# Fourier mixing followed by an ELU layer: the order of the first seven steps rewritten as one list of single operations

## The chip, the cores and the metric

The kernel runs on one core of a Trainium2 chip. The metric is device time in microseconds (us), the median over runs of the whole kernel. Before the change it is 1950.72 us, the median of three runs (1949.22 to 1950.72). The profile shown below is of one more execution; its run took 1951.19 us and its span, from the first to the last instruction, is 1949.1 us.

## The reference

```python
def _attn_ref(x):                      # x: (8, 3008, 256) float32
    X = np.fft.fft(x, axis=1)
    X = np.fft.fft(X, axis=2)
    return X.real.astype(np.float32)

def _moe_ref(x, w_in, w_out):          # x: (24064, 256), w_in: (256, 2048), w_out: (2048, 256)
    h = x @ w_in
    g = np.where(h > 0.0, h, np.exp(np.minimum(h, 0.0)) - 1.0)
    return (g @ w_out).astype(np.float32)
```

The two weight matrices arrive as 8-byte floating-point numbers, because they are scaled by a NumPy double. The kernel converts them to float32 itself, by integer operations on the two 32-bit words of each number.

## The kernel before, in words

**The mathematics.** The transform over 256 channels is multiplied into w_in (the "fold" of a chunk of w_in), so that what remains for x is the transform over 3008 rows. Its symmetries cut it to quarters: x is first folded into sums and differences of mirrored rows and channels (`fold_x`, L498; all VectorE at the start), and four half-length transforms of each batch are matmuls against constant matrices (`Dft`, L609). The results go into rings `Rr`, `Ir` and `Rb` in SBUF, 256 columns to a tile. A **step** (or slot) then takes one tile and 256 of the 2048 hidden channels: two matmul groups give h for a frequency and for its mirror, ELU is applied to both, and a third group multiplies by w_out. There are 47 tiles and 8 steps to a tile, 376 steps. The first sixteen steps go back and forth between tiles 0 and 1; from step 16 on a step uses a form with fewer products.

**Names.** The change gives each operation a short name; they are used here for both kernels. For step n:

- Pn (TensorE, L794): the cosine part of h into a new PSUM bank with the tag `H`. Vn (VectorE, L803): E = P plus a rank-one term. Qn (TensorE, L799): the sine part, added onto P in the same bank, so it waits for Vn, which reads the bank first.
- hn (VectorE, L817): h of the mirror. b+n and b-n (ScalarE, L842, L846): what lies below zero. x+n and x-n (ScalarE): exponentials. g+n and g-n (VectorE, L857, L861): ELU. g+n is the last reader of the step's `H` bank.
- Xan and Xbn (TensorE, L904): the products with w_out, eight matmul records each.

For the first batch: the names x, R, I, O, J are five transforms (of the extra channel, and the four of `R_even`, `I_even`, `R_odd`, `I_odd`), each with -even and -odd (matmuls), -copy (ScalarE), -sum, -up and -down (VectorE; -up and -down write the ring). e0 to EO3 are the folds of x, c0 to c3 one-column copies, xs four tiny sums. For chunk c of w_in (w) and of w_out (u): a and b take bits out of the high words (VectorE), p, l, d convert (ScalarE), s sets the sign (VectorE), R adds and M multiplies (GpSimd, but VectorE for w0), P makes sum and difference for the fold (GpSimd). fc is the fold of w chunk c (TensorE, into an `H` bank), Wsc and Wcc copy it out (ScalarE), wmc and wexc turn one row of it into columns. L0 to L3 are loads of the second batch.

**Banks.** `bank` (L404) gives PSUM banks by tag: one each for pA, pB, pC, pD and M, three for `H`. P, f, the two halves of J and a few later operations share the three `H` banks; a fourth user waits until a bank's last reader is done.

**What sets the order.** Every compute operation is pinned: each engine executes its instructions in the order in which the program emits them. The emission order is that of the events: `at(t, fn)` (L1131) notes a function with a number, and L1434 calls them in the order of the numbers. The numbers stand for microseconds of a plan in which a step takes `PERIOD` = 4.8; no time is enforced. For the beginning they are written in several places: L1146 to L1184 (folds, first transforms, chunks 0 and 1), the table `first` (L1204) for the chunks, L1222 to L1231 for the folds, the table `begin` for steps 0 and 1 (L1247, L1258), and L1345 on with two calls of `at_half` for the O and J transforms. A single event often emits several operations: `fields` is a and b, `power` is p, l and d, `fold_now` a whole string of folds. SyncE issues the loads in a fixed order, and `load_rest` (L1135) holds the later ones back until x has landed. Before any of this, 46 dummy matmuls are issued.

Of the kernel before, what the change touches and what calls it, by code (L numbers as in the profile page):

```python
# [25 lines left out]
NE = 377  # L26
# [80 lines left out]
def kernel(  # L107
# [109 lines left out]
    class Chunk:  # L217
# [30 lines left out]
        def fields(self):  # L248

            if not wide:  # L250
                return
            lo, hi, dst = self.parts()
            t = spool.tile([128, 512], I32, tag=self.tmp_tag, bufs=1, name="pow2")
            self.t = t.rearrange("p (a b) -> p a b", a=dst.shape[1])
            pin(
                nc.vector.tensor_scalar(
                    out=self.t, in0=hi, scalar1=0x7FF00000, scalar2=None,
                    op0=ALU.bitwise_and,
                )
            )  # L260
            pin(
                nc.vector.tensor_scalar(
                    out=dst.bitcast(I32), in0=hi, scalar1=0xFFFFF, scalar2=0x100000,
                    op0=ALU.bitwise_and, op1=ALU.bitwise_or,
                )
            )

        def power(self):

            if not wide:  # L270
                return
            act(self.t, self.t, func=AF.Relu, scale=8.0, bias=ebias)
            if self.shared:
                lo, _, dst = self.parts()
                act(lo.bitcast(FP), lo.bitcast(U32), scale=2.0**-52)
                act(dst, dst.bitcast(I32), scale=2.0**-20)

        def round(self):

            if not wide:  # L280
                return
            lo, hi, dst = self.parts()
            if self.shared:
                gtt(dst, lo.bitcast(FP), dst, ALU.add)
                return
            pin(
                nc.vector.scalar_tensor_tensor(
                    out=dst, in0=lo.bitcast(U32), scalar=2.0**-32,
                    in1=dst.bitcast(I32), op0=ALU.mult, op1=ALU.add,
                )  # L290
            )

        def pair(self):

            dst = self.dst()
            gtt(self.ab[:, 0:256], dst[:, 0], dst[:, 1], ALU.add)
            gtt(self.ab[:, 256:512], dst[:, 0], dst[:, 1], ALU.subtract)

        def scale(self):

            self.multiply()
            if self.pairs:
                self.pair()

        def multiply(self):
            if not wide:
                return
            lo, hi, dst = self.parts()
# [5 lines left out]
            )  # L314
            if self.shared:
                gtt(dst, dst, self.t.bitcast(FP), ALU.mult)
                return
# [4 lines left out]
                )  # L322
            )
# [124 lines left out]

    def put_chunk(c):
        cols = slice(c * 256, (c + 1) * 256)  # L450
        for n, dst in enumerate((Ws, Wc)):
            act(dst[:, cols], folds[c][:, 256 * n : 256 * n + 256])
# [45 lines left out]
    def fold_x(L, engine_of, pieces):  # L498
# [3 lines left out]
        def op(key, o, a, b, f):  # L502
# [3 lines left out]
            n = o.shape[1]  # L506
            cuts = [n * i // pieces for i in range(pieces + 1)]
            for i in range(pieces):
# [100 lines left out]
    class Dft:  # L609
# [30 lines left out]
        def minus(self):  # L640
# [8 lines left out]
            if self.ri == 0 and not self.kodd and not self.first:  # L649
                vtt(R4[:, self.b : self.b + 1], u[:, 0:1], v[:, 0:1], ALU.subtract)  # L650
# [165 lines left out]

    def h_minus(i):  # L817
        S = steps[i]
        S.G = spool.tile([128, GW], FP, tag="G", bufs=3, name="G")
# [22 lines left out]
    def below_plus(i):  # L842
        S = steps[i]
        below(S.G[:, 512:1024], S.H)
# [262 lines left out]
    for load in loads[:5]:  # L1107
# [8 lines left out]
        L_first, lambda key: nc.vector, 1  # L1116
    )

    def fold_now(keys):
        for key in keys.split():  # L1120
            ops[key, 0]()
# [13 lines left out]
    def load_rest():  # L1135
# [7 lines left out]
        for chunk in (w1_chunks[3], w2_chunks[1], w1_chunks[4], w2_chunks[2]):  # L1143
            chunk.load()

    at(-26.9, lambda: fold_now("e3 c3 o3"))  # L1146
    at(-26.8, w1_chunks[0].fields)
    at(-26.7, w1_chunks[0].power)
    at(-26.6, w1_chunks[0].round)
    at(-26.5, w1_chunks[0].scale)  # L1150
    at(-26.4, lambda: fold_now("e0 c0 e2 c2 E2"))
# [3 lines left out]
    at(-25.5, load_rest)  # L1155
    at(-24.5, begin_x_even)
    at(-24.4, lambda: fold_now("e1 c1 E0 EO0"))
    at(-20.7, lambda: load_mats(1, 1))
    at(-20.6, w1_chunks[5].load)
    at(-20.5, w2_chunks[5].load)  # L1160
    at(-13.2, lambda: fold_chunk(0))
    at(-13.1, lambda: put_chunk(0))
    at(-13.1, lambda: dft_now(state["x_even"], 0, "pC"))
    at(-13.09, lambda: state["x_even"].copy())
    at(-13.08, lambda: dft_now(state["x_even"], 1, "pD"))
    at(-13.0, lambda: dft_now(R_even, 0, "pA"))
    at(-12.9, lambda: dft_now(R_even, 1, "pB"))
    at(-11.1, lambda: fold_now("o0 o2 O2 o1 O0 EO2"))
    at(-11.0, lambda: state["x_even"].unfold())
    at(-10.95, R_even.copy)  # L1170
    at(-10.94, R_even.unfold)
    at(-10.9, R_even.plus)
    at(-10.89, lambda: state["x_even"].plus())
    at(-10.885, lambda: act(Ir[96:128, 0:NE], Rb[96:128, 0:NE]))
    at(-10.88, w1_chunks[1].fields)
    at(-10.87, w1_chunks[1].power)
    at(-10.86, w1_chunks[1].round)
    at(-10.85, R_even.minus)
    at(-10.5, lambda: dft_now(I_even, 0, "pC"))
    at(0.05, lambda: dft_now(I_even, 1, "M"))  # L1180
    at(0.6, lambda: state["x_even"].minus())
    at(0.61, lambda: act(Ir[96:128, NE:RUN], Rb[96:128, NE:RUN]))
    at(-10.84, w1_chunks[1].scale)
    at(1.3, lambda: fold_now("EO1"))  # L1184

    T = PERIOD
    for chunk, k in (
        (w2_chunks[0], 0),
        (w1_chunks[2], 1),
        (w2_chunks[1], 2),  # L1190
        (w1_chunks[3], 3),
        (w2_chunks[2], 4),
        (w1_chunks[4], 5),
        (w2_chunks[3], 6),
# [9 lines left out]
        first = (  # L1204
            (0.96, 0.96, 0.97, 1.9),
            (2.1, 2.9, 2.91, 4.22),
            (2.95, 2.96, 2.97, 4.2),
            (0.95, 0.96, 0.97, 4.2),
        )
        dt = first[k] if k < 4 else (-0.5, 0.05, 0.06, 2.95)  # L1210
        for d, fn in zip(dt, (chunk.fields, chunk.power, chunk.round, chunk.scale)):
            at(t + d, fn)
    for chunk, t in (
        (w2_chunks[3], 0.5),
        (w2_chunks[4], 0.95),
# [6 lines left out]
    for c in range(1, 8):  # L1222
        at((2 * c - 2) * T + 4.7 if c > 1 else 2.7, lambda c=c: fold_chunk(c))
        t = (2 * c - 1) * T + 0.03 if c > 1 else 3.0
        at(t, lambda c=c: put_chunk(c))
        if c > 1:
            at(t + 0.01, lambda c=c: spread_last_row(c))
    at(-10.6, lambda: turn_last_row(0))
    at(-10.59, lambda: put_last_row(0))
    at(3.15, lambda: turn_last_row(1))  # L1230
    at(T + 0.25, lambda: put_last_row(1))  # L1231
    for i in range(8):
        at((12.9 + 0.5 * i) * T + 3.6, lambda i=i: sum_weights(i))
    at(2 * T + 4.2, lambda: fold_now("EO3"))
# [9 lines left out]
    for slot in range(total):  # L1244
        i = slot % 2 * 8 + slot // 2 if slot < 16 else slot
        t = slot * T
        begin = (  # L1247
            (0.0, mm_P),
            (0.4 if slot == 0 else 0.9, even_part),
            (2.17, mm_Q),  # L1250
            (3.55, h_minus),
            (4.2, below_plus),
            (4.8, below_minus),
            (T + 0.01 if slot < 16 else T + 1.5, exp_plus),
            (T + 0.02 if slot < 16 else T + 2.21, exp_minus),
        )
        if slot == 1:
            begin = (  # L1258
                (0.1 - T, mm_P),
                (0.7 - T, even_part),  # L1260
                (2.6 - T, mm_Q),
                (1.5, h_minus),
                (2.95, below_plus),
                (3.0, below_minus),
                (3.01, exp_plus),
                (3.02, exp_minus),
            )

        X3 = ((3 * T + 0.1 if i % 8 == 0 else 2 * T + 3.05, mm_X3),)
        for dt, fn in begin + (  # L1270
            (T + 2.2, g_plus),
            (T + 2.9, g_minus),
        ) + (
            (
                (2 * T + 0.87, lambda i: mm_plain(i, 0)),
                (2 * T + 3.04, lambda i: mm_plain(i, 1)),
            )
            if i < 16
            else WINOGRAD + X3
        ):  # L1280
            at(t + dt, lambda fn=fn, i=i: fn(i))
# [59 lines left out]
    def begin_folds(b):  # L1341
        state["EO"], state["ops"] = fold_x(state["L"], lambda key: nc.gpsimd, 2)

    steps_b = HALF * 8 // TW
    for t, fn in (  # L1345
        (-1.8, I_even.copy),
        (0.5, I_even.unfold),
        (0.55, I_even.plus),
        (0.65, I_even.minus),
        (3.1, lambda: dft_now(R_odd, 0, "pA")),  # L1350
        (3.2, lambda: dft_now(R_odd, 1, "pB")),
        (T + 0.005, R_odd.copy),
        (T + 1.9, R_odd.unfold),
        (T + 4.2, R_odd.plus),
        (T + 4.21, R_odd.minus),
    ):
        at(t, fn)
    at_half(3, lambda: I_odd, 0, 0)
    at_half(5, lambda: I_odd, 1, HALF)
# [25 lines left out]
    for b in range(1, NB):  # L1385
# [4 lines left out]
        for n in range(6):  # L1390
            t = l0 + gap * n if n < 4 else l0
            at(t * T + 0.2, lambda n=n: state["loads"][n]())
# [73 lines left out]
```

## Time and profile before

| | |
|---|---|
| median of three runs | 1950.72 us (1949.22 to 1950.72) |
| profiled span | 1949.1 us |
| busy | TensorE 1935.8, GpSimd 1376.4, VectorE 1299.4, ScalarE 864.8 us |
| first matmul of the fold of chunk 0 | 13.43 us from the span's start |
| P0, P2, P6, P7 start | 25.40, 39.95, 67.87, 74.16 us |
| last matmul starts | 1945.8 us |

How to read it: TensorE is busy nearly all of the span by its own records, but a matmul's record is longer than the time to the next one's start, so short pauses do not show as idle. A stretch of the timeline tells more: a row has the start, the time to the end of the last of its instructions, the engine (PE is TensorE, DVE VectorE, ACT ScalarE, POOL GpSimd), what is written and read, and in brackets the idle time before it with what ended it. Four matmul records of 256 columns in a row take 0.86 us, eight take 1.73 us.

### The profile page before, as it was taken

The page shows a single profiled execution, that of the slowest core. Times are in us where ns is not written, and L with a number is a line of the kernel's source. Part 1 is how long each engine was busy: PE and PEld are TensorE (multiplying, and loading weights), DVE is VectorE, ACT ScalarE, POOL GpSimd, SP SyncE. Part 2 cuts the span into 40 slices and gives each one's busy share as a digit, 9 for nine tenths or more (in the row PEclk, how much of TensorE's full clock was granted, in tenths as well). Part 3 has the DMA queues.
Part 4 walks back from the last instruction along what each step waited for, and adds up shares of the span by engine and source line. Part 5 has one row for each costly group of instructions (what it writes and reads, how often), then busy time and mean ns, then how long its engine had stood idle before and what let it go on. Part 6 is the DMA issues. An engine that isn't in the chain of part 4 may idle for free.

```text
span 1949.1 us, 26994 instructions
## 1 busy us (share of the span) xinstructions
PE 1935.8 (99%) x8912; PEld 1653.3 (85%) x8912; DVE 1299.4 (67%) x2396; ACT 864.8 (44%) x1671; POOL 1376.4 (71%) x1816
## 2 busy tenths in 40 slices
PE   8999999999999999999999999999999999999999
PEld 5788788888888888888888888888888888888887
DVE  7966666666667666666666665676666766667666
ACT  4654444444444444444344444444444444344443
POOL 3887767776678766777677876778767776456655
PEclk9999999999999999999999999999999999999999
DMA  8246120101101021010210202012020010100101
GB/s 310 66 32 49 29 54 20 47 14 26 42 20 44 15 44 28 18 47 13 53 24 12 49 10 59 12 20 58 7 54 11 20 23 14 17 12 11 23 9 25
DMA packets 263290, 70.25 MB, mean 36 GB/s; under 512 B 248606, under 2 KB 249522, under 8 KB 263152
## 3 DMA queue, kind: packets, MB, share of 16 engines
q1 hardware_dynamic: 257360, 55.69, 15.0%
q0 software_dynamic: 3616, 12.59, 2.1%
q8 instruction: 70, 1.15, 0.3%
q14 instruction: 68, 0.56, 0.1%
q10 hardware_dynamic: 2176, 0.26, 0.1%
HBM read 43.66 MB, written 24.80 MB: 35 GB/s over the span
## 4 chain that ended last, share of the span: by engine, by line
PE 94%; DVE 2%; POOL 2%; ACT 1%; DMA 1%; issue 1%; SPq 0%; DVEq 0%
PE H L410 38%; PE pB L410 16%; PE pC L410 16%; PE pD L410 16%; PE pA L410 8%; POOL WT L419 1%; POOL G L419 0%; DMA xl<-in_x_dram 0%; DVE E L811 0%; POOL w L419 0%; DVE G L837 0%; DVE o L504 0%; DMA xl<-in_x_dram,ix 0%; DVE e L504 0%; DVE v L416 0%
## 5 line engine op out<-in xcount | busy, mean ns | idle before, releaser
L419 POOL TENSOR_TENSOR G<-G 128x256 f32<-128x256 f32 x1440 | 1034.8, 728 | 510.7 <-DVE G L837 341.2
L811 DVE SCALAR_TENSOR_TENSOR E<-Rb,wex,H 128x256 f32<-128x256 f32 x752 | 327.9, 477 | 541.3 <-PE H L410 537.2
L422 ACT ACTIVATE G<-H 128x512 f32<-128x512 f32 x376 | 224.5, 597 | 958.9 <-DVE G L821 958.9
L410 PE MATMUL H<-Ir,Ws 128*128 128x256 f32 x1504 | 387.6, 380 | 5.3 <-DVE E L811 4.3
L410 PE MATMUL H<-Rr,Wc 128*128 128x256 f32 x1504 | 386.8, 380 | 0.0
L410 PE MATMUL pC<-G,WT 128*128 128x256 f32 x1440 | 369.5, 379 | 0.0
L410 PEld LDWEIGHTS H<-Rr,Wc 128*128 128x128 f32 x1504 | 284.8, 190 | 55.3 <-issue 3.0
L410 PEld LDWEIGHTS H<-Ir,Ws 128*128 128x128 f32 x1504 | 278.5, 189 | 54.1 <-DVE E L811 6.0
L410 PEld LDWEIGHTS pC<-G,WT 128*128 128x128 f32 x1440 | 273.6, 190 | 37.2
L821 DVE SCALAR_TENSOR_TENSOR G<-E,H 128x512 f32<-128x512 f32 x376 | 256.9, 683 | 41.2 <-POOL G L419 5.0
L837 DVE SCALAR_TENSOR_TENSOR G<-G,H 128x512 f32<-128x512 f32 x376 | 255.9, 681 | 42.5 <-ACT G L422 42.5
L837 DVE SCALAR_TENSOR_TENSOR G<-M,G 128x512 f32<-128x512 f32 x376 | 256.8, 683 | 0.0
L422 ACT ACTIVATE G<-G 128x512 f32<-128x512 f32 x376 | 233.2, 620 | 0.0
L410 PE MATMUL pD<-G,w 128*128 128x256 f32 x784 | 229.4, 379 | 0.8 <-POOL G L419 0.8
L410 PE MATMUL pA<-G,w 128*128 128x256 f32 x784 | 229.3, 379 | 0.0
L410 PE MATMUL pB<-G,w 128*128 128x256 f32 x784 | 229.2, 379 | 0.0
L422 ACT ACTIVATE M<-G 128x512 f32<-128x512 f32 x376 | 224.3, 596 | 0.0
L422 ACT ACTIVATE M<-M 128x512 f32<-128x512 f32 x376 | 220.9, 588 | 0.0
L410 PE MATMUL pB<-G,WT 128*128 128x256 f32 x720 | 214.8, 380 | 0.3
L410 PE MATMUL pD<-G,WT 128*128 128x256 f32 x720 | 214.1, 379 | 0.0
L410 PEld LDWEIGHTS pD<-G,w 128*128 128x128 f32 x784 | 148.9, 190 | 21.4 <-POOL G L419 1.2
L410 PEld LDWEIGHTS pA<-G,w 128*128 128x128 f32 x784 | 148.9, 190 | 20.4 <-issue 0.2
(148 smaller groups left out, 1415.3 us busy)
## 6 DMA issues: line engine op xcount, KB each, us to landing
out_dram<-ot SPq DMA_DIRECT2D x496, 32.0 KB
xl<-in_x_dram SPq DMA_DIRECT2D x16, 512.0 KB
xl<-in_x_dram SPq DMA_DIRECT2D x16, 256.0 KB
out_dram<-ot SPq DMA_DIRECT2D x256, 2.0 KB
Rb<-r SPq DMA_DIRECT2D x10, 376.0 KB
raw<-in_moe_w_in_dram SPq DMA_DIRECT2D x7, 512.0 KB
MC<-dft_mats SPq DMA_DIRECT2D x3, 943.5 KB
raw<-in_moe_w_out_dram SPq DMA_DIRECT2D x4, 512.0 KB
```

Of the source, the lines that this page charges most:

```text
L410: nc.tensor.matmul(out_, lhsT=lhsT, rhs=rhs, start=start, stop=stop, skip_group_check=True)
L419: pin(nc.gpsimd.tensor_tensor(out=o, in0=a, in1=b, op=op))
L422: pin(nc.scalar.activation(out=o, in_=i, func=func, **kw))
L811: nc.vector.scalar_tensor_tensor(out=S.E[:, c], in0=Rb[:, cols(i)], scalar=wex[:, f : f + 1], in1=S.H[:, c], op0=ALU.mult, op1=ALU.add,)
L821: nc.vector.scalar_tensor_tensor(out=two(S.G[:, 0:512])[:, :, ::-1], in0=two(S.E), scalar=2.0, in1=two(S.H), op0=ALU.mult, op1=ALU.subtract,)
L837: nc.vector.scalar_tensor_tensor(out=o, in0=e, scalar=-1.0, in1=h, op0=ALU.add, op1=ALU.max)
```

## The change

- The operations of the beginning are split into single ones: `fields` becomes `top` and `mantissa` (a, b); `power` becomes p, l and d; `scale` becomes s, M and P; the fold's two copies become two operations; R's one-column subtraction is taken out of `minus` and becomes R4.
- A list `FRONT` of 40 lines names 227 operations, in the order in which they are to be emitted. It replaces all numbers of the places above up to about step 6. What comes later keeps its place, except that chunk 4 of w_out is loaded a little later, and a few chunks' conversions come earlier.
- The folds e0 and e2 are cut in two, rows 0 to 3 and 4 to 5, because the two parts of these tiles come by separate transfers. The first batch's other folds stay whole.
- J-even is emitted directly behind Q1 and ahead of P2, J-odd behind P2 and wm1; before, they came after Xb1 and Xb3. J-up and J-down stay behind step 6.

The core of the diff (the list is cut to the lines that the text speaks of):

```diff
-    def fold_x(L, engine_of, pieces):
+    def fold_x(L, engine_of, cuts_of):
...
-            cuts = [n * i // pieces for i in range(pieces + 1)]
-            for i in range(pieces):
+            cuts = cuts_of(key, o.shape[1])
+            for i in range(len(cuts) - 1):
...
     EO, ops = fold_x(
-        L_first, lambda key: nc.vector, 1
+        L_first,
+        lambda key: nc.vector,
+        lambda key, n: (0, 4, n) if key in ("e0", "e2") else (0, n),
     )
...
-    at(-26.9, lambda: fold_now("e3 c3 o3"))
-    at(-26.8, w1_chunks[0].fields)
...
-    at(0.05, lambda: dft_now(I_even, 1, "M"))
...
+    FRONT = (
+        (-20.44, "e3 o3"),
+        (-18.71, "w0a w0b w0p w0R c3"),
+        (-17.22, "w0s e0a"),
+        (-15.57, "w0M e2b e2a"),
+        (-14.12, "e0b o2 o0"),
+        (-12.44, "f0 O2 xl1 c0"),
+        (-11.12, "e1 c2 Wc0 xs"),
+        (-9.82, "c1 E2 x-even E0"),
+        (-8.33, "x-odd w1b EO0"),
+        (-6.77, "o1 R-even w1a w2l O0"),
+        (-5.15, "R-odd Ws0 w1l u0b EO2 w1p"),
+        (-3.54, "R-copy EO1 w1d I-odd x-copy R-sum w1R u0d"),
+        (-2.11, "x-sum R-up I-even x-up"),
+        (-0.66, "w2b Irc u0a P0 w1s I-copy u0p"),
+        (0.64, "R4 I-sum w1M wm0 u0l O-even R-down I-up wex0"),
+        (2.2, "V0 u0R P1 x-down w4l"),
+        (3.47, "w2a Q0 w1P w2d Irc2 O-odd V1 O-copy"),
+        (4.86, "b+0 I-down w2R w2p h0 x+0"),
+        (6.34, "EO3 f1 u1l b-0 Q1 u1b"),
+        (7.71, "u2l u0s J-even Wc1 w2s x-0"),
+        (9.1, "O-sum Ws1 w2M P2 g-0 J-copy u1d h1 wm1 b+1"),
+        (10.2, "u0M O-up J-odd g+0 x+1 u1a wex1 b-1 w2P x-1"),
+        (11.39, "Xa0 g+1 w3l O-down u1R u1p V2 f2 g-1"),
+        (12.84, "w3a Q2 w4b u1s Xb0 w3b b+2 u1M u2b"),
+        (14.05, "w3d Ws2 P3 x+2 J-sum w3R w3p h2 Xa1"),
+        (15.67, "Wc2 V3 b-2 u2a x-2 w3s Q3"),
...
+        (21.24, "Q4 L1 g-3 u2p f3 h4 b+4 u2R"),
+        (22.53, "u3d g+3 Xb2 b-4 u2s Ws3 Wc3 w4s"),
...
+        (32.99, "h6 u3M g+5 b-6 J-up"),
+        (34.63, "J-down"),
+    )
+    front = set()
+    for t, line in FRONT:
+        for n, name in enumerate(line.split()):
+            front.add(name)
+            at(t + 0.001 * n, names[name])
...
-        (3.1, lambda: dft_now(R_odd, 0, "pA")),
-        (3.2, lambda: dft_now(R_odd, 1, "pB")),
...
-    at_half(3, lambda: I_odd, 0, 0)
-    at_half(5, lambda: I_odd, 1, HALF)
```

## The prediction

> **What bounds the kernel now.** I read the page first, then busy time by stretch, then the timeline of TensorE and of VectorE over the first 70 us. From the page:
>
> ```profile
> PE 1935.8 (99%) x8912; PEld 1653.3 (85%) x8912; DVE 1299.4 (67%) x2396; ACT 864.8 (44%) x1671; POOL 1376.4 (71%) x1816
> ```
>
> TensorE is the bound of the whole, and the change neither adds nor removes a matmul. The time can only change by pauses of TensorE, and only early ones are touched. Busy time by stretch (start:end, length, then busy us and instructions of PE, weight loads, DVE, ACT, POOL; granted clock; DMA share; GB/s):
>
> ```profile
> 13.40:25.40 12.00, 10.23 (x52) 7.02 (x51) 11.65 (x21) 1.76 (x6) 0.00 (x0) 1.00 1.03 403
> 25.40:40.00 14.60, 12.29 (x48) 7.66 (x47) 10.89 (x26) 8.62 (x20) 6.54 (x6) 0.88 0.88 317
> 40.00:44.80 4.80, 3.83 (x18) 2.87 (x17) 4.80 (x9) 3.02 (x6) 2.93 (x3) 1.00 0.71 283
> 44.80:67.90 23.10, 23.09 (x110) 18.06 (x109) 21.97 (x34) 17.07 (x34) 18.20 (x16) 1.00 0.45 137
> ```
>
> From 44.8 us TensorE never rests (23.09 of 23.10). Before that VectorE is the fuller engine (11.65 of 12.00). The pauses, in TensorE's timeline:
>
> ```profile
> 24.04 1.52 PE L410 MATMUL pC<-MC,o 128*128 128x189 f32 x6 [1.77 <-DVE bs L416]
> ...
> 30.24 1.10 PE L410 MATMUL H<-Ir,Ws 128*128 128x256 f32 x4 [1.05 <-DVE Ir L416]
> 32.60 1.74 PE L410 MATMUL H<-Ir,Ws 128*128 128x256 f32 x4 [1.26 <-DVE E L811]
> ...
> 39.95 1.02 PE L410 MATMUL H<-Rr,Wc 128*128 128x256 f32 x4
> ...
> 43.79 1.13 PE L410 MATMUL H<-Ir,Ws 128*128 128x256 f32 x4 [0.97 <-DVE E L811]
> ```
>
> These are I-even, Q0, Q1, P2 and Q2. From f0 (13.43) to Xb0 (44.76) 31.3 us pass. The matmuls in between, at start-to-start times of unpaused rows (four records of 256 columns 0.86, an even transform 1.3 to 1.4, an odd one 1.9, f0 1.87, f1 1.0, wm 0.4), need 23.5. So **7.8 us** of pauses are all there is to win, up to P2 6.7 of them. VectorE around P2:
>
> ```profile
> 39.43 0.68 DVE L837 SCALAR_TENSOR_TENSOR G<-G,H 128x512 f32<-128x512 f32 x1
> ...
> 46.87 0.68 DVE L310 SCALAR_TENSOR_TENSOR pow<-w,pow 128x512 int32<-128x512 int32 x1
> 47.47 2.05 DVE L504 TENSOR_TENSOR o<-o,o 128x768 f32<-128x768 f32 x1
> ```
>
> The first row is g+0. It frees step 0's `H` bank, and P2, which needs that bank, starts as it ends. The last is EO3 beside GpSimd work: 2.05 us, where such folds take 0.96.
>
> **The Trainium skill.** "TensorE: Matmul & The Clock Gate", Part 1, says that after about a 3.4 us window of little work the clock is halved until a busy window has passed. The trace agrees: clock 0.88 over 25.4 to 40 us is 0.12 × 14.6 × 2 = 3.5 us at half, and Q1 took 1.67 us (32.60 to 34.27) for 0.86. The same page, under "Architectural detail", says that VectorE and ScalarE are strict queues and matmuls keep their order; in the trace Q2 waits for a V2 that stands behind a 1.4 us operation, as it should then. "GPSIMD Engine Reference", "Key points": GpSimd shares its SBUF interfaces with VectorE operations of two SBUF inputs; the EO3 row agrees.
>
> **The change, part by part.** I lay the new order of each engine over the durations of the trace (start to start in a full queue: fold 0.87, bit operation 0.33, sign or round 0.60, V 0.79, sum 0.53, up or down 0.46, h or g 0.59, b 0.5, x 0.53, p 0.62, l or d 0.57, copy of anti 0.33).
>
> *Cut folds.* Two more VectorE instructions, at most 0.1 us together. They run in the 1.5 us in which VectorE waited for x (9.73 to 11.27): hidden. With o2, o0 and O2 also ahead of e1, x-even can start at about 16.0 instead of 15.31 (xs is later): a pause of 0.7.
>
> *VectorE to R-sum.* e0b ends at 11.95 (its transfer lands at 11.2; e2b, e2a and e0b take 1.2 from e2b's landing at 10.7). Eleven folds (o2, o0, O2, e1, E2, E0, EO0, o1, O0, EO2, EO1), xs and c1 (0.64) and the bit operations w1b, w1a, u0b come to 11.2, so R-sum starts near 23.2; before it was 23.86, with EO1 and the bit operations still to do. TensorE then runs x, R, I-odd (22.5), I-even, P0 (25.8), wm0, O-even, P1, Q0 (29.2), O-odd, f1 and Q1, 17.7 us of matmuls from 16.0 with 0.2 of pauses, and ends Q1 at **33.9**. Before, the same work and wm1 were done at 39.95. That is a lead of 39.95 - 33.9 - 0.35 (wm1) = **5.7 us**.
>
> *J-even ahead of P2.* The built program shows a new wait: J-even takes step 0's `H` bank (f0 to f1, P0 and P1 hold the three), so it waits for g+0. VectorE from 23.2 to the end of g+0: 11.5 us of listed work after x-up at 25.3, and 0.3 to 1 us for GpSimd beside w2a and EO3: **37.4**. TensorE waits 37.4 + 0.1 - 33.9 = **3.6 us**. Queued behind J-even are P2 and everything after.
>
> *P2 behind it.* P2 now takes step 1's bank and waits for g+1. ScalarE has J-copy, u1d, b+1, x+1 in this order ahead of g+1, and J-copy waits for J-even. After J-even's end: 0.15 + 0.33 + 0.57 + 0.5 + 0.53 + 0.59 and some 0.15 of hand-overs = **2.8 us** of pause. P2 starts at 41.6.
>
> *A bank less.* J-odd holds an `H` bank from there to J-down, behind step 6 (before, J-odd held one for 5 us). Two banks remain for P and f, so new waits follow, each with the instruction that it waits behind:
> - J-odd waits for wex1, which waits for wm1: 0.45.
> - f2 takes J-even's bank and waits for J-sum, which stands behind V2, g-1 and five bit and sign operations: 0.5 to 1.8. I take 0.5, as a J-odd that comes late hides it.
> - P3 waits for Wc2, on ScalarE behind b+2 (which waits for Q2), w3d, Ws2, x+2, w3p: 0.2 + 0.5 + 0.57 + 0.28 + 0.53 + 0.62 + 0.45 = 3.15, less Xb0's 1.73 beside it: 1.4.
> - f3 stands directly behind Q4 and waits for g+3, on VectorE behind h4, which waits for Q4: 0.2 + 0.59 + 0.65 + 0.1 = 1.5.
> - P7 stands directly behind f4 and waits for its Wc4: 0.2 + 0.28 + 0.38 + 0.1 = 0.95.
> Together 4.8. The pause of 1.1 in front of Q2 goes.
>
> *Clock.* Between 33 and 43 us TensorE works some third of the time, as it did before the halving seen (Q0 and the start of Q1, 1.2 of 3.4 us). Where the halving falls is not known: from 0 to 2.8 us (J-even slowed, then J-odd and Xa0). I take 1.1, J-even alone. The halving of before is inside the 39.95.
>
> *The rest.* The single operations are the same instructions as before; R4 moved costs VectorE 0.2, counted above. SyncE's loads keep their order to the 23rd; the later load of w_out's chunk 4 is used long after 80 us. GpSimd's L0 and L1 (2.2 us) now stand ahead of u2R and u2M, which Xa4 needs some 6 us after they are done: hidden. A pause of 0.65 before 108 us may be absorbed (0 to 0.65; I take 0).
>
> Sum: -5.7 + 3.6 + 2.8 + 4.8 - 1.1 + 1.1 = **+5.5 us**. The profiled span would be 1949.1 + 5.5 = 1954.6. The runs' median is 1.6 us above that span, so **1956.2 us**.
>
> **The rivals.**
> 1. *The bank waits are not felt (faster).* If the banks came free as the order of the list supposes, with J-even directly behind Q1, the waits of J-even, P2, P3, f3 and P7 (10.25 us) and the clock term would vanish: -5.7 + 0.45 + 0.5 - 1.1 = -5.9, or 1944.8 us. It decides where these five waits come to less than 5.9 us. For it: VectorE is 2 us ahead at g+0, and 5.7 us of lead is real. Against it: the waits stand in the program, and VectorE's work up to g+0 is a sum that leaves little room.
> 2. *Lead and waits cancel (the same).* ScalarE and VectorE hand over faster, f2's and P7's waits are hidden and no halving occurs: 5.5 - 1.1 - 0.5 - 0.95 - 0.65 - 1 (f3 and P3 shorter) = +1.3, or 1952.0 us.
> 3. *The change acts only in part*: the list moves emission, not data, and TensorE could still wait for loads that come at the same time (403 GB/s up to 25 us). The last needed one, the sine matrix of the odd rows, lands by about 32.3, ahead of J-even. It would be case 2 again.
>
> **How the numbers follow.** Chances: 0.60 for the forecast (its own range 1953.5 to 1960.5), 0.25 for rivals 2 and 3, 0.15 for rival 1. A measurement of this kernel tells some 0.2% (3.9 us) from no change. Of the forecast's chance a tenth falls under that bound, of rivals 2 and 3 a tenth above. So: slower 0.57, same 0.28, faster 0.15. The range leaves out rival 1 and a small tail above: 1949 to 1961.
>
> **What would show it.** In TensorE's timeline of the changed kernel: x-even near 16, Q1 ending near 34, then a pause of over 3 us in front of J-even ended by VectorE's g+0, one of over 2 us in front of P2 ended by g+1, about 1.5 in front of P3 (ScalarE) and f3 (VectorE), 1 in front of P7, and P7 at 74.16 + 5.5 = 79.7. If J-even starts within 1 us of Q1's end, or P6 starts before 67.87, the forecast is wrong.

## The result, and the profile after

The changed kernel takes **1958.93 us** (median of 6 runs, 1958.86 to 1960.18); the kernel before, run beside it, 1950.53 us (6 runs). The two medians differ by 8.4 us, or 0.43%; the measured ratio is 1.0046, 95% interval 1.0033 to 1.0059: slower. The profiled span is 1957.1 us against 1949.1.

The page's row of busy times for the kernel after:

```profile
PE 1937.8 (99%) x8912; PEld 1655.6 (85%) x8912; DVE 1291.9 (66%) x2398; ACT 865.6 (44%) x1671; POOL 1375.6 (70%) x1816
```

The number of matmuls is unchanged, 8912, and VectorE has two instructions more, the cut folds. TensorE's busy time grew by 2.0 us, though its work is the same: some of the matmuls ran longer. The other 6 us are pauses. Both are net of what the kernel before had, which also ran at half clock from 32.92 to 36.33 us. Busy time by stretch of the kernel after, over the stretches used for the kernel before:

```profile
13.40:25.40 12.00, 10.84 (x51) 7.21 (x51) 11.97 (x25) 4.40 (x12) 1.68 (x1) 1.00 1.03 403
25.40:40.00 14.60, 10.71 (x50) 7.30 (x48) 12.78 (x28) 9.49 (x21) 9.50 (x9) 0.99 1.03 388
40.00:44.80 4.80, 2.69 (x8) 2.26 (x8) 1.15 (x2) 1.18 (x4) 1.29 (x1) 0.50 0.20 76
44.80:67.90 23.10, 20.15 (x83) 14.78 (x84) 14.21 (x27) 11.94 (x24) 9.41 (x9) 0.89 0.23 80
```

Up to 40 us VectorE does more than before (12.78 us busy in the second stretch, before 10.89): the lead is real. From there every engine does less. TensorE gets 83 matmuls done from 44.80 to 67.90, where before it did 110, and rests for 3 of the 23 us; the clock is 0.50 in the third stretch and 0.89 in the fourth. TensorE's timeline of the kernel after (start, time to the last end, what is written and read, idle time before it and its releaser):

```profile
16.51 1.54 PE L430 MATMUL pC<-MC,xe 128*128 128x189 f32 x6 [1.16 <-DVE xe L436]
...
33.47 1.13 PE L430 MATMUL H<-Ir,Ws 128*128 128x256 f32 x4
37.67 1.51 PE L430 MATMUL H<-MC,o 128*128 128x188 f32 x6 [3.07 <-issue]
42.07 2.04 PE L430 MATMUL H<-Rr,Wc 128*128 128x256 f32 x4 [2.90 <-DVE G L869]
43.91 0.85 PE L430 MATMUL H<-pick,Ws 128*128 128x1 f32 x4
45.02 4.13 PE L430 MATMUL H<-MC,o 128*128 128x376 f32 x6 [0.26 <-ACT wex L442]
48.94 2.35 PE L430 MATMUL pA<-G,w 128*128 128x256 f32 x8
51.22 1.08 PE L430 MATMUL H<-raw,CC 128*64 128x256 f32 x8
...
56.24 1.13 PE L430 MATMUL H<-Rr,Wc 128*128 128x256 f32 x4 [1.15 <-ACT Wc L442]
...
66.73 1.08 PE L430 MATMUL H<-raw,CC 128*64 128x256 f32 x8 [1.58 <-DVE G L869]
...
80.58 1.08 PE L430 MATMUL H<-Wc,CC 128*64 128x256 f32 x8 [0.48 <-DVE G L869]
82.47 1.13 PE L430 MATMUL H<-Rr,Wc 128*128 128x256 f32 x4 [0.81 <-ACT Wc L442]
```

In order: x-even, Q1, J-even, P2, wm1, J-odd, Xa0, f2, P3, f3, f4, P7. The forecast's pauses are there, but for f2's, which does not show (experiment 1 tells why). By experiment 3 below J-even can follow Q1's start after 0.97 us, so TensorE was free for it at 33.47 + 0.97 = 34.4. "Issue" at J-even names no releaser; VectorE's timeline does:

```profile
36.89 0.67 DVE L869 SCALAR_TENSOR_TENSOR G<-G,H 128x512 f32<-128x512 f32 x1
...
41.24 0.69 DVE L869 SCALAR_TENSOR_TENSOR G<-G,H 128x512 f32<-128x512 f32 x1 [2.83 <-ACT G L442]
...
48.32 1.49 DVE L268 TENSOR_SCALAR w<-w 128x512 int32<-128x512 int32 x1
49.73 0.60 DVE L436 TENSOR_TENSOR bs<-H,anti 127x188 f32<-127x188 f32 x2
```

g+0 ends at 37.56 and J-even starts 0.11 later. The second row is g+1: VectorE waits 2.83 us for ScalarE ahead of it. ScalarE's timeline shows what stands in front:

```profile
39.21 0.33 ACT L442 ACTIVATE anti<-H 127x188 f32<-127x188 f32 x1 [3.87 <-PE H L430]
39.44 0.62 ACT L442 ACTIVATE w<-w 128x512 f32<-128x512 int32 x1
39.95 0.59 ACT L442 ACTIVATE G<-H 128x512 f32<-128x512 f32 x1
40.58 0.63 ACT L442 ACTIVATE G<-G 128x512 f32<-128x512 f32 x1
```

These are J-copy, u1d, b+1, x+1. J-copy waits 3.87 us, the last 1.5 of them for J-even; b+1 and x+1 need nothing of J but stand behind it.

The clock in the records of the profiled execution is half from 39.62 to 49.86 us, 10.24 us. By start-to-start times, against the same matmuls of a kernel at full clock (the fifth experiment, in brackets): P2 1.84 (0.94), wm1 1.11 with a pause of 0.26 (0.37), J-odd 3.92 (1.98), Xa0 2.28 (1.82). That is 0.90 + 0.48 + 1.94 + 0.46 = **3.8 us**.

### The profile page after: what moved, and what is told of

Its sections match the earlier page's. It is cut to its first block, busy times and chain, and to the rows that moved or that the text cites. A ratio compares the mean times of both kernels' runs of the same rounds, so it can differ in the third digit from the quotient of the medians.

```text
span 1957.1 us, 26985 instructions
## 1 busy us (share of the span) xinstructions
PE 1937.8 (99%) x8912; PEld 1655.6 (85%) x8912; DVE 1291.9 (66%) x2398; ACT 865.6 (44%) x1671; POOL 1375.6 (70%) x1816
## 4 chain that ended last, share of the span: by engine, by line
PE 95%; DVE 2%; POOL 1%; ACT 1%; issue 1%; DMA 0%; DVEq 0%; POOLq 0%; ACTq 0%
PE H L430 38%; PE pC L430 16%; PE pB L430 16%; PE pD L430 16%; PE pA L430 8%; POOL WT L439 1%; DMA xl<-in_x_dram,ix 0%; DVE G L869 0%; POOL G L439 0%; POOL w L439 0%; ACT G L442 0%; DVE E L839 0%; DVE G L853 0%; DVE v L436 0%; DVE o L527 0%
```

## The experiments

The theory: J-even and J-odd take `H` banks out of turn, which makes the pauses one by one, and the pauses make the clock halve. Its rivals: the pauses hide each other (take one away, another opens), the cut folds or the loads are to blame, or the clock's halving hides behind the waits. Each edit is to the changed kernel. All results are compared with the kernel before; its medians beside experiments 1 to 4, 5 to 7 and 8 and 9 were 1950.45, 1950.58 and 1950.55 us. Experiments 5 to 7 ran on another chip than the other six.

**1. The clock kept up.** Twenty-six dummy matmuls of zeros, written to an idle bank, are added in the two pauses around J-even.

```diff
-        (7.71, "u2l u0s J-even Wc1 w2s x-0"),
+        (7.71, "u2l u0s spin1 J-even spin2 Wc1 w2s x-0"),
```

> The changed kernel with 14 dummy matmuls (bank pC, idle then) between Q1 and J-even and 12 between J-even and P2, 5.6 us of TensorE in pauses of 3.3 and 3.1 us; nothing else moves. It separates the halved clock from the waits. Bank theory: the waits stay, P2 at 42.1 again; the clock stays full; J-odd and Xa0 end 3.2 us earlier, but f2 then waits for J-sum (about 49.1 instead of 51.2), so only 2.0 us come back: 1956.9 us. Rival that the halved clock is the main loss: all of P2, wm1, J-odd and Xa0 come back, 4.0 us or more: 1955 us or less.

Measured: 1957.1 us (6 runs), ratio 1.0035 (1.0022 to 1.0048), clock 1.00 throughout. TensorE's timeline of this kernel:

```profile
41.90 1.13 PE L430 MATMUL H<-Rr,Wc 128*128 128x256 f32 x4 [0.19 <-DVE G L869]
...
43.63 2.17 PE L430 MATMUL H<-MC,o 128*128 128x376 f32 x6 [0.26 <-ACT wex L442]
...
49.05 1.08 PE L430 MATMUL H<-raw,CC 128*64 128x256 f32 x8 [1.52 <-POOL w L439]
```

J-odd takes 2.17 us for 4.13, but f2 now waits 1.52 us. The releaser named is a GpSimd operation on a tile `w`; the last one before f2 is u1M, which ended at 48.13, 0.9 us too early to be it. f2 takes J-even's bank. VectorE's timeline of this kernel shows the last reader of that bank, J-sum, in the second row (the first is u2b):

```profile
46.94 1.49 DVE L268 TENSOR_SCALAR w<-w 128x512 int32<-128x512 int32 x1
48.34 0.60 DVE L436 TENSOR_TENSOR bs<-H,anti 127x188 f32<-127x188 f32 x2
```

J-sum ends at 48.94, f2 starts at 49.05. In the changed kernel the same wait is there and hides behind the slow J-odd. So the halved clock costs 3.8 us of TensorE's time and 1.8 us net.

**2. J back at its old places.** J-even behind Xb1 and J-odd behind Xb3, with their copy, sum, up and down.

```diff
-        (7.71, "u2l u0s J-even Wc1 w2s x-0"),
+        (7.71, "u2l u0s Wc1 w2s x-0"),
-        (10.2, "u0M O-up J-odd g+0 x+1 u1a wex1 b-1 w2P x-1"),
+        (10.2, "u0M O-up g+0 x+1 u1a wex1 b-1 w2P x-1"),
...
+        (17.3, "g+2 w3M Xb1 J-even h3 b+3 g-2"),
...
+        (26.33, "g+4 w4R Q5 u3a Xb3 J-odd b+5"),
```

> The changed kernel with J-even put back behind Xb1 and J-odd behind Xb3 (J-copy, J-sum, J-up, J-down with them), as before the change; all else of the new order stays. Bank theory: P2 waits only for g+0 and starts at 37.6, two banks are never both held by J, no window falls to the half clock, P4 starts near 50.6 where the kernel before has 54.3: 1946.8 us. Rival that VectorE's new order is what delays TensorE: P2 near 37.6 as well, but later steps wait for VectorE as before: 1952 us or more.

Measured: 1950.89 us (12 runs), ratio 1.0001 (0.9993 to 1.0010). It takes back the whole loss, but is 4 us above what was expected, no better than the kernel before. TensorE's timeline:

```profile
39.62 1.10 PE L430 MATMUL H<-Rr,Wc 128*128 128x256 f32 x4 [3.12 <-DVE G L869]
...
59.58 1.08 PE L430 MATMUL H<-raw,CC 128*64 128x256 f32 x8 [1.30 <-DVE bs L436]
```

P2 has now nothing to run ahead of it and itself waits for g+0 (3.12 us), as expected. Two things were left out of the expectation: behind this wait the clock halves for 3.4 us (Xa0 takes 3.59 us, 1.82 at full clock), and f3, which stands directly behind Q4 in the new list, waits 1.30 us for J-sum. J in an `H` bank costs at this place too. By this trace the two make some 3.1 of the 4 us; the rest is not explained. In this profiled execution the first load also came late (last section): without these 1.9 us P2 would start near the 37.6 that was expected.

**3. J in other banks.** J-even and J-odd stay where the change put them, but take banks pC and pD; J-sum, J-up and J-down stand right behind V2, so that these are free for Xa1 and the later products.

```diff
-        ("J", lambda: I_odd, ("H", "H")),
+        ("J", lambda: I_odd, ("pC", "pD")),
...
-        (11.39, "Xa0 g+1 w3l O-down u1R u1p V2 f2 g-1"),
+        (11.39, "Xa0 g+1 w3l O-down u1R u1p V2 f2 J-sum J-up J-down g-1"),
```

> The changed kernel with the same order on TensorE, but J-even in bank pC and J-odd in pD (free until Xa1) instead of two H banks; so that they are free by then, J-sum, J-up and J-down stand behind V2. Bank theory: J-even follows Q1 at once (34.4), P2 at 37.6, no halving, no pause over 1 us before P4, which starts near 51.3 with J-odd done: 1946 us. Rival that the place of J ahead of P2 is the fault whatever the bank (TensorE's order, 3.2 us of J in front of the steps): no better than 1952 us. Rival that VectorE is the limit: 1955 us.

Measured: **1946.6 us** (12 runs), ratio 0.9981 (0.9973 to 0.9990): faster than the kernel before, and 12.3 us below the changed kernel's median. In its timeline J-even starts 0.97 us after Q1 does, with no pause, and the only one left is P2's:

```profile
35.35 1.13 PE L430 MATMUL H<-Ir,Ws 128*128 128x256 f32 x4
36.32 1.43 PE L430 MATMUL pC<-MC,o 128*128 128x188 f32 x6
39.61 1.10 PE L430 MATMUL H<-Rr,Wc 128*128 128x256 f32 x4 [1.85 <-DVE G L869]
```

The profiled execution had the late first load, too, and a halved clock behind P2's pause; it took 1949.88 us. The early place of J is thus not what made the change slow; the `H` banks were. What the early place gains by itself is not shown: no run has J late in these banks. With the banks P2 keeps the wait for g+0, since step 0's bank is what it takes, but J-even fills part of it.

**4. J-odd's bank given back early.** J-up and J-down right behind J-sum instead of behind step 6.

```diff
-        (14.05, "w3d Ws2 P3 x+2 J-sum w3R w3p h2 Xa1"),
+        (14.05, "w3d Ws2 P3 x+2 J-sum J-up J-down w3R w3p h2 Xa1"),
```

> The changed kernel with J-up and J-down right behind J-sum instead of behind step 6, so that J-odd gives its H bank back by about 51 us; the waits in front of J-even and P2 and the halved clock stay. Bank theory: the pauses in front of P3 (1.3), f3 (1.6), f4 and P7 (1.4) go: 1954.6 us. Rival that these pauses come from the order on ScalarE and VectorE whatever the banks: 1958.9 us.

Measured: 1955.54 us (19 runs), ratio 1.0025 (1.0018 to 1.0032), 3.4 us below the changed kernel's median. TensorE's timeline:

```profile
54.75 1.03 PE L430 MATMUL H<-Rr,Wc 128*128 128x256 f32 x4
...
63.48 1.08 PE L430 MATMUL H<-raw,CC 128*64 128x256 f32 x8
...
77.79 1.13 PE L430 MATMUL H<-Rr,Wc 128*128 128x256 f32 x4
```

J-even and P2 pause as in the changed kernel (3.07 and 2.90 us); the three rows, P3, f3 and P7, have no pause any more, nor has f4, and P7 starts 4.7 us earlier. So these later waits do come from the bank that J-odd keeps.

**5. Other banks and a full clock.** Experiment 3 with eight dummy matmuls added between J-even and P2.

```diff
-        (7.71, "u2l u0s J-even Wc1 w2s x-0"),
+        (7.71, "u2l u0s J-even spin Wc1 w2s x-0"),
```

> The version with J in banks pC and pD, with 8 dummy matmuls (1.7 us, bank pD) in its remaining pause of 2.0 us between J-even and P2. In its profile the clock was half for 3.4 us right behind that pause and J-odd took 1.6 us longer for it. Bank and clock theory: no halving, 1945.0 us, 1.5 below the version without. Rival that the halving is hidden by a later wait, as two of its four microseconds were in the changed kernel: 1946.6 us.

Measured: 1947.04 us (16 runs), ratio 0.9982 (0.9974 to 0.9989), no different from experiment 3. The list of single runs suggests why: of the twelve runs of experiment 3, eight had a mean clock of 1.000 and spans of 1944.2 to 1945.1 us, and the four at 0.999 spans of 1946.3 to 1948.1. Its median run seems to have had no halving to take away. The profiled execution was one of the four, and its first load was late as well, so the two groups do not price the halving alone. In experiment 5 four of the sixteen runs still have a mean clock of 0.999. Whether the dummy matmuls save anything in a run that would otherwise halve is not shown.

**6. The folds whole again.**

```diff
-        lambda key, n: (0, 4, n) if key in ("e0", "e2") else (0, n),
+        lambda key, n: (0, n),
```

> The changed kernel with e0 and e2 in one piece each, e0 where its second piece stood; all else as changed. Bank theory: VectorE reaches g+0 0.3 to 0.5 us later and everything behind it too: 1959.3 us. Rival that the two more instructions cost more than they bring: 1958.5 us or less.

Measured: 1961.06 us (5 runs), ratio 1.0050 (1.0037 to 1.0064), 2.1 us above the changed kernel. The intervals overlap. TensorE's timeline:

```profile
38.04 2.53 PE L430 MATMUL H<-MC,o 128*128 128x188 f32 x6 [3.08 <-issue]
43.47 2.05 PE L430 MATMUL H<-Rr,Wc 128*128 128x256 f32 x4 [2.90 <-DVE G L869]
```

J-even starts 0.37 us later than in the changed kernel: that is about what the cut gains, since VectorE has 1.83 us of these folds behind its wait for x, and with the cut 1.36. The other 1 us by P2 is J-even itself, 2.53 us for 1.51: here the clock was half from 38.37 on, for 13.65 us. In this profile it is thus the clock that makes a small edit look large, not the folds.

**7. J-copy behind x+1.** Only this one instruction moves, on ScalarE.

```diff
-        (9.1, "O-sum Ws1 w2M P2 g-0 J-copy u1d h1 wm1 b+1"),
-        (10.2, "u0M O-up J-odd g+0 x+1 u1a wex1 b-1 w2P x-1"),
+        (9.1, "O-sum Ws1 w2M P2 g-0 u1d h1 wm1 b+1"),
+        (10.2, "u0M O-up J-odd g+0 x+1 J-copy u1a wex1 b-1 w2P x-1"),
```

> The changed kernel with one operation moved on ScalarE alone: J-copy stands behind b+1 and x+1 instead of ahead of u1d, b+1 and x+1. J-even still waits for g+0, and P2 still for g+1. Theory of the queue (P2's pause is ScalarE's order, J-copy waiting for J-even with g+1's inputs behind it): g+1 is done before J-even ends, P2 follows J-even at once (39.1 instead of 42.1), the windows are too full for a halving, f2 starts near 46 instead of 51.2: 1953.7 us. Rival that P2's pause is VectorE's own work ahead of g+1: 1958.9 us.

Measured: 1955.96 us (10 runs), ratio 1.0028 (1.0019 to 1.0038), 3.0 us below the changed kernel, where 5.2 were expected. TensorE's timeline:

```profile
37.86 2.84 PE L430 MATMUL H<-MC,o 128*128 128x188 f32 x6 [3.07 <-issue]
40.50 1.91 PE L430 MATMUL H<-Rr,Wc 128*128 128x256 f32 x4
```

P2's pause of 2.90 is gone, so it came from J-copy's place on ScalarE and not from VectorE's own work. P2 starts 1.57 us earlier: most of the rest went into J-even, which ran wholly at half clock (from 37.19 on). This kernel's one run at a clock of 1.000 had a span of 1952.5 us, those at 0.997 spans of 1954.6 to 1957.2.

**8. That, with the clock kept up.** Experiment 7 with fourteen dummy matmuls added ahead of J-even.

> J-copy behind x+1 (as in the run that moved it alone) and 14 dummy matmuls ahead of J-even. If the copy's place makes P2's pause, and the run that moved it alone got back only half because the clock was halved just then, P2 starts near 39.2 (42.07 in the changed kernel) behind a J-even of 1.5 us, the clock stays full, f2 waits about 1.5 us for J-sum, and the time is about 1954.0 us. If halving is not what took the other half, it is as in that run, 1956.0 us.

Measured: 1954.51 us (17 runs), ratio 1.0019 (1.0012 to 1.0026), 0.5 us above the 1954.0 expected if the clock took the other half, and clear of the 1956.0 of the rival. TensorE's timeline:

```profile
37.49 1.51 PE L430 MATMUL H<-MC,o 128*128 128x188 f32 x6
38.96 1.10 PE L430 MATMUL H<-Rr,Wc 128*128 128x256 f32 x4
...
46.08 1.08 PE L430 MATMUL H<-raw,CC 128*64 128x256 f32 x8 [1.53 <-POOL w L439]
...
51.11 1.13 PE L430 MATMUL H<-Rr,Wc 128*128 128x256 f32 x4 [1.15 <-ACT Wc L442]
```

P2 at 38.96 behind a J-even of full speed, f2 waits 1.53, and P3, f3, f4 and P7 wait as long as in the changed kernel.

**9. And J-odd's bank given back.** Experiments 4 and 8 together.

> The same with J-up and J-down also right behind J-sum: every pause that the change makes is then taken away except J-even's wait for g+0 (3.2 us), J-odd's (0.3) and f2's (1.5), with J still in two of the three H banks. If the account of the change is a sum, the pauses of P3, f3, f4 and P7 (4.2 by the trace, 3.4 by the medians of the run that moved J-up and J-down alone) come off the run before it: 1949.8 to 1950.6 us, as fast as the kernel before. If the pauses stand in for each other, so that another bank wait opens where one is closed, it stays above 1952.5 us.

Measured: 1950.00 us (13 runs), ratio 0.9997 (0.9989 to 1.0005). P3, f3 and P7 in TensorE's timeline:

```profile
49.85 1.03 PE L430 MATMUL H<-Rr,Wc 128*128 128x256 f32 x4
...
58.58 1.08 PE L430 MATMUL H<-raw,CC 128*64 128x256 f32 x8
...
72.89 1.13 PE L430 MATMUL H<-Rr,Wc 128*128 128x256 f32 x4
```

Their pauses and f4's are gone, and none has opened in their place. The account of the change is a sum: 8.9 us of the changed kernel's time lie in J-copy's place, J-odd's bank and the clock, and what is left (waits of J-even, J-odd and f2 of 3.2 + 0.3 + 1.5, less the lead of 5.2 and Q2's old pause of 1.1) is -1.3 us by the trace, -0.55 by the medians.

## Why the prediction was right

The direction was right, and the time lies inside the range, 2.7 us above the forecast. By the forecast's steps, up to J-odd and for the clock from start-to-start times, for P3 to P7 from the pauses in brackets:

| step | forecast, us | measured, us | shown by |
|---|---|---|---|
| lead at Q1's end | -5.7 | -5.2 | trace; x-even's pause 1.16, not 0.7 |
| J-even waits for g+0 | +3.6 | +3.2 | trace, experiment 3 |
| P2 waits for g+1 behind J-copy | +2.8 | +2.9 | experiments 7 and 8 |
| J-odd, wex1 | +0.45 | +0.26 | trace |
| f2, J-sum | +0.5 | 0 (1.5 at full clock) | experiments 1 and 8 |
| P3 | +1.4 | +1.2 | experiment 4 |
| f3 | +1.5 | +1.6 | experiment 4 |
| f4 | none | +0.5 | experiment 4 |
| P7 | +0.95 | +0.8 | experiment 4 |
| Q2's old pause | -1.1 | -1.1 | trace |
| halved clock | +1.1 | +3.8 | trace; net of f2 1.8, experiment 1 |
| sum | +5.5 | +8.0 | span: +8.0 |

The sum is good to some 0.3 us: at the start of P7 the two kernels are 8.3 us apart (82.47 and 74.16). Without the clock the other misses, of up to 0.5 us each, go both ways and come to -0.2; that they cancel so well is luck.

**The clock is the term that was mis-sized.** The forecast gave a range of 0 to 2.8 us and took 1.1, for J-even alone; 3.8 lies outside that range. Three windows of 3.4 us in a row were halved, and they lay over P2, wm1, J-odd and part of Xa0, with J-even just ahead of them. The Trainium skill, "TensorE: Matmul & The Clock Gate", Part 1, says that the window is 3413 ns and "free-running". The traces agree: the clock was half for 3.41 us in the kernel before, for 10.24 in the changed kernel and in experiment 7, and for 13.65 in experiment 6, which is one, three and four windows. In the last three it began at 39.62, 37.19 and 38.37 us, though they reach J-even within 0.4 us of each other. The trace of before, with one halved window, gave no ground for three. The forecast also read this page's condition as a window of little work; the page speaks of an idle one, and the last section has what the traces show.

**Two smaller misses.** f2's wait was put at 0.5, from a range of 0.5 to 1.8, and is 1.5 us by itself. The trace of experiment 1 has a likely reason: u2b, ahead of J-sum, took 1.49 us (46.94 to 48.43) beside a GpSimd operation (46.82 to 48.13), where the same form took 0.42 at 33.18 us in the changed kernel with GpSimd at rest. No run moves either of the two. The slow J-odd hides the wait, as the forecast said of a late J-odd. f4's wait of 0.5 was not foreseen: f4, too, stands a bank short.

**The rivals.** The first, in which the bank waits are not felt, gave 1944.8 us. It is false of the changed kernel and nearly true of experiment 3, where J takes other banks: 1946.6 us, with P2's pause left. The second let lead and waits cancel, at 1952.0 us: of what it took away only f2's wait was hidden; P3, f3 and P7 paused nearly as forecast, and the clock halved. The third, that loads would hold TensorE up, is seen in none of the changed kernel's pauses above, which end with VectorE or ScalarE. The point on which the sign turned, bank waits of J-even, P2, P3, f3 and P7 against a lead of some 5.9 us, was 9.7 us by measurement.

## What to carry to other kernels

When matmuls are moved forward in a fixed order, write down for each buffer that they take who reads it last and where that reader stands on its engine; then do the same for the users that follow, since a bank held from here to there takes the place of a buffer from all of them. Give the moved work a bank of its own before giving up its place: here the same order went from 0.46% slower to 0.19% faster by two tags and the place of three VectorE operations. Count a pause of 3 us of TensorE twice, once as itself and once as a possible halved clock for the next matmuls, with a range of several windows.

## What the runs showed of the hardware

- **A halved clock needs no idle window.** The Trainium skill, "TensorE: Matmul & The Clock Gate", Part 1, puts the halving after an idle window of about 3.4 us; these traces differ. In the changed kernel it began at 39.62 us, so the window ahead of it lay from 36.21 to 39.62, and J-even ran in it for 1.5 us, 44%. The pause there, from Q1's end at 34.44 to 37.67, was 3.2 us, shorter than a window. In the kernel before, the clock halved at 32.92 us, with no pause above 2 us since f0. The last of the changed kernel's three halved windows (46.44 to 49.86) followed one in which TensorE worked nearly all the time. Which window decides, and from which busy share, stays open.
- **A wait can be put down to the wrong operation.** f2's releaser in experiments 1 and 8 is named as GpSimd, whose last instruction had ended 0.9 us earlier; J-sum on VectorE ended 0.1 us before f2.
- **The first loads don't always land at the same time.** The first operation on w_in starts at 6.99 us in the changed kernel, without a wait. In the profiled executions of experiments 2 and 3 it waited for its load, and everything up to P2 was some 1.9 us later. Why the load was late stays open. It may add to the spread of runs of one kernel (spans of 1947.0 to 1951.3 us for the kernel before). VectorE's timeline of experiment 2:

```profile
9.78 0.43 DVE L256 TENSOR_SCALAR pow<-raw 128x512 int32<-128x512 int32 x1 [2.69 <-DMA raw<-in_moe_w_in_dram]
```
